# Attention's exponential on VectorE with five equally weighted terms and one V, more buffers for its bits, and the MLP's x plus bias formed on GpSimd

## The chip, the cores and the metric

One Trainium2 chip, one core. The metric is the device time of one execution in microseconds (us), of which the median over several runs counts.

## What is computed

Tokens x (1 x 2048 x 512) go through a layer norm; the result feeds two branches in parallel, and their outputs are added to x:

```python
xn = _layernorm(x, axis=-1)
return x + _A_ref(xn, A_wqkv, A_wo) + _B_ref(xn, B_w1, B_b1, B_w2, B_b2)
```

A is softmax attention with 32 heads of 16 columns (scores scaled by 1/4, no mask), B is an MLP that norms xn once more, 512 to 1792 columns with a tanh GELU, and back to 512 with bias b2.

## The kernel before

**Tiles and groups.** The 32 heads make 8 sets of 4 (HS), the 2048 queries 4 blocks of 512 (QW). A pair of query block and head set is a group g; there are 32 (NG), taken in order. In a group there are 16 key tiles k of 128 keys, and for each k and each of the 4 heads one unit: the scores of 128 keys by 512 queries, one PSUM bank. 32 x 16 x 4 = 2048 units.

**Two engines for the exponential.** TensorE computes scores (`qk`, L1054), for 2 or 3 units in one go that fill banks 0 to 3 in turn. ScalarE takes the exponential of such a tile in one instruction (`fex`, L1237) into `p_sb`, and TensorE multiplies it with V (`pv`, L1072), four heads side by side in the columns of the array: four matmuls of 128 x 32 weights, called a pack below. V has a column of ones per head, so the softmax sum comes out with the product. A further unit can ride along with a tile's scores into another bank (`ride`); it belongs to VectorE. `build_dve` makes the instructions: `f1` (L1319) adds LEVEL to scaled scores, clips at 0 and writes int16, whose bits read as f16 are a rough exponential; `f2` (L1343) adds a constant SHIFT[t] to the bits of all four heads of a key tile, four times, which shifts the place where the roughness lies. The five f16 arrays are multiplied with V and with four copies of V that are scaled by WEIGHT[t] (`vs`, written in `scaled`, L938), and all five products add up in the group's PSUM bank. So a key tile on VectorE costs four `f1`, four `f2` and 20 value matmuls, where one on ScalarE costs four.

**Which unit goes where.** KD lists the key tiles that may go to VectorE: (2, 5, 8, 11, 14) of each group from g = 2 on. `next_d` hands one over when fewer than OUT tiles are under way; what VectorE doesn't take, ScalarE takes at the group's end (`take_unit`). In groups 0 and 1, which run beside the projections, only tile 8 of group 1 goes to VectorE.

**Buffers.** `ib` has NI = 3 slots for a key tile's converted scores, all in `x_sb`, whose tokens are no longer needed; `tb` has NTB = 3 slots for shifted bits. All of them pass in turn.

**The rest.** Keys, queries and V are projected on the way (`project`, `vmm`); for the key tiles of KD but tile 5 the V projection is computed a second time, later, only to write `vs`. Per query block the MLP runs as `build_mlp` (up, bias on VectorE at L1498, GELU on ScalarE at L1508) and `build_down`: per 128 tokens a chain of 16 steps on TensorE through `chain` (L597), one that adds the tokens by a product with the identity, 14 for w2, and one that adds b2 as ones times a row; VectorE copies the result to the accumulator `acc` (L1531, in the memory of `wkv`). `build_out` multiplies the normalised heads with wo, adds `acc` (L1553) and stores. GpSimd has little: constants, the square roots of the norm, and per group four small instructions (L1398 to L1404) that check the softmax sums when they come back from memory as `lc`.

**What sets the order.** No engine chooses at run time. A planner in the program (`_Plan.run`) holds for every operation a cost, a due time (`prio`) and its dependencies, and writes out one fixed order per engine: of the operations that could start, the one due first. Groups are due RATE + 1.1 us apart. In gaps of TensorE's plan it inserts matmuls with zeros (`fill`, L1630), which keep its clock up. A change of a cost, of a slot count or of RATE so moves instructions everywhere.

## Time and profile before

| what | value |
|---|---|
| time, median of 3 runs (lowest to highest) | 817.85 us (816.5 to 818.91) |
| profiled execution, span from first to last instruction | 814.1 us |
| the same execution's own time, by the median's distance | some 3.75 us above its span |
| instructions | 23268 |

The profile is of one execution of its own. Its span runs from the first to the last instruction; what lies around the span isn't in it. Busy time of TensorE is modelled, since matmuls overlap; instructions of VectorE and ScalarE also overlap at their ends, so that the mean of one is longer than the distance from one to the next.

### The profile page before, as it was taken

What the parts mean: (1) busy time and instruction counts of PE and PEld (TensorE: products, weight loads), DVE (VectorE), ACT (ScalarE), POOL (GpSimd) and SP (SyncE); (2) the same over time, 40 slices, a digit from 0 to 9 for tenths busy, and PEclk for the clock granted to TensorE, in tenths of its full rate; (3) what the DMA queues carried; (4) which work ended last, traced back from release to release, by engine and by line L of the source; (5) the groups of instructions that cost most, each with busy time, mean ns of one, the idle gap of its engine ahead of it and who ended that gap; (6) DMA issues with size and microseconds to landing.
All of it is one profiled execution on the core that took longest, in us unless ns stands there. A gap on an engine that the chain in (4) does not pass through costs nothing.

```text
span 814.1 us, 23268 instructions
## 1 busy us (share of the span) xinstructions
PE 780.0 (96%) x9887; PEld 260.7 (32%) x9888; DVE 751.4 (92%) x1304; ACT 775.5 (95%) x676; POOL 57.5 (7%) x165
## 2 busy tenths in 40 slices
PE   8999999999999999999999999999999999999997
PEld 3333332333332333333333333233332333333332
DVE  8959999997899999997999999899899999999885
ACT  6779999999999999999999999899999999999995
POOL 3300001001000000000000000000100010000001
PEclk9999999999999999999999999999999999999999
DMA  6210031101010011200002011100000101211001
GB/s 188 92 22 2 18 84 30 35 15 30 15 30 15 25 45 41 54 22 10 16 16 40 23 35 42 48 21 22 23 16 16 28 16 41 61 42 28 12 23 34
DMA packets 54798, 27.99 MB, mean 34 GB/s; under 512 B 40613, under 2 KB 50598, under 8 KB 54690
## 3 DMA queue, kind: packets, MB, share of 16 engines
q1 hardware_dynamic: 52818, 25.03, 11.3%
q8 instruction: 78, 1.28, 0.7%
q10 hardware_dynamic: 1872, 1.44, 0.6%
q14 instruction: 30, 0.25, 0.1%
HBM read 23.85 MB, written 2.61 MB: 32 GB/s over the span
## 4 chain that ended last, share of the span: by engine, by line
DVE 42%; PE 40%; ACT 10%; issue 7%; DMA 1%; DVEq 0%; ACTq 0%; SPq 0%
DVE x_sb L1319 16%; PE ps L597 14%; PE ps L1072 13%; PE ps L1054 12%; DVE tb_x L1343 10%; ACT p_sb L1237 8%; DVE x_sb L1343 4%; DVE ht L1498 2%; DVE osb L1377 1%; DVE stats L728 1%; ACT ht L1508 1%; DVE qc L918 1%; PE ps L1630 1%; DVE qz L923 1%; DMA ldram<-osb 1%
## 5 line engine op out<-in xcount | busy, mean ns | idle before, releaser
L1237 ACT ACTIVATE p_sb<-ps 128x1024 bf16<-128x1024 f32 (+1 forms) x649 | 734.0, 1251 | 21.6 <-PE ps L1054 10.2
L1054 PE MATMUL ps<-qz,kt 32*128 32x512 bf16 x2048 | 311.0, 383 | 18.6 <-ACT p_sb L1237 6.5
L1319 DVE TENSOR_SCALAR x_sb<-ps 128x512 int16<-128x512 f32 x456 | 301.1, 680 | 21.1 <-PE ps L1054 19.5
L1343 DVE TENSOR_SCALAR tb_x<-x_sb 128x2048 int16<-128x2048 int16 x304 | 202.5, 680 | 1.8 <-PE ps L1072 1.2
L1054 PEld LDWEIGHTS <-kt 32*128 32x128 bf16 x2048 | 85.0, 91 | 276.3 <-issue 269.4
L1072 PE MATMUL ps<-p_sb,va 128*32 128x512 bf16 x1592 | 157.4, 390 | 0.3 <-DVE osb L1377 0.3
L1072 PE MATMUL ps<-tb_x,vs 128*32 128x512 f16 x1216 | 111.7, 382 | 1.1 <-DVE tb_x L1343 0.9
L1343 DVE TENSOR_SCALAR x_sb<-x_sb 128x2048 int16<-128x2048 int16 x152 | 103.5, 681 | 4.1 <-PE ps L1072 3.5
L1072 PEld LDWEIGHTS <-va 128*32 128x32 bf16 x2048 | 49.7, 93 | 107.2 <-issue 103.9
L1072 PEld LDWEIGHTS <-vs 128*32 128x32 bf16 x1824 | 50.3, 96 | 44.1 <-issue 23.6
L1398 POOL TENSOR_SCALAR okt<-lc 128x16 f32<-128x16 f32 x31 | 11.3, 363 | 701.2 <-DMA lc<-ldram 701.2
L597 PE MATMUL ps<-yT,w_r 128*32 128x512 bf16 x896 | 59.2, 384 | 1.6 <-DVE ht L1498 0.8
L1072 PE MATMUL ps<-x_sb,vs 128*32 128x512 f16 x608 | 59.6, 381 | 0.7 <-DVE x_sb L1343 0.6
L597 PE MATMUL ps<-w_sb,ht 128*32 128x512 bf16 x896 | 59.6, 380 | 0.0
L1072 PE MATMUL ps<-x_sb,va 128*32 128x512 f16 x456 | 45.1, 385 | 1.5 <-DVE x_sb L1319 1.2
L1498 DVE TENSOR_SCALAR ht<-ps,b_sb 128x512 bf16<-128x512 f32 x56 | 41.4, 739 | 2.3 <-PE ps L597 2.2
L1630 PE MATMUL ps<-ones_bf,zeros_bf 128*32 128x512 bf16 x416 | 36.8, 384 | 0.0
L597 PE MATMUL ps<-wo_pad,ont 128*32 128x512 bf16 x512 | 33.9, 380 | 0.5 <-DVE ont L1427 0.2
L597 PEld LDWEIGHTS <-w_r 128*32 128x32 bf16 x896 | 22.7, 96 | 25.6 <-issue 11.5
L597 PEld LDWEIGHTS <-ht 128*32 128x32 bf16 x896 | 21.7, 96 | 21.7 <-issue 5.7
L1508 ACT ACTIVATE ht<-ht 128x3584 bf16<-128x3584 bf16 x8 | 25.1, 3183 | 0.0
L1377 DVE COPY osb<-ps 128x512 f32<-128x512 f32 x31 | 21.1, 680 | 0.5 <-PE ps L1072 0.3
(100 smaller groups left out, 362.3 us busy)
## 6 DMA issues: line engine op xcount, KB each, us to landing
rlb<-rdram SPq DMA_DIRECT2D x31, 256.0 KB
w_r<-in_B_w_dram SPq DMA_DIRECT2D x56, 128.0 KB
x_r<-in_A_x_dram SPq DMA_DIRECT2D x16, 128.0 KB
w_sb<-in_B_w_dram SPq DMA_DIRECT2D x1, 1792.0 KB
out_dram<-ot SPq DMA_DIRECT2D x12, 128.0 KB
x_sb<-in_A_x_dram SPq DMA_DIRECT2D x2, 512.0 KB
wkv<-in_A_wqkv_dram ACTq DMA_DIRECT2D x1, 512.0 KB
x_sb<-in_A_x_dram ACTq DMA_DIRECT2D x1, 512.0 KB
```

What stands on the lines that cost most here:

```text
L597: I(nc.tensor.matmul(dst[32 * j:32 * j + 32], lhsT=lhsT[:, 32 * j:32 * j + 32], rhs=rhs, start=start, stop=stop, tile_position=(0, 32 * j)))
L728: I(nc.vector.bn_stats(out=stats[:, t, :], in_=x_sb[:, t, :]))
L1054: I(nc.tensor.matmul(ps[:, bank, :], lhsT=kt[lo:lo + 32, s // 2, k * P:(k + 1) * P], rhs=qz[lo:lo + 32, (qt * NB + s // 2) % NQB, s % 2, : ...
L1072: I(nc.tensor.matmul(ps[32 * j:32 * j + 32, o_bank[g], :], lhsT=vals[:, h * VS:h * VS + 32], rhs=wts(j), start=pv_done[g] == 1, stop=end, ...
L1237: I(nc.scalar.activation(p_sb[:, s0:s1, :].rearrange("p a b -> p (a b)"), ps[:, b0:b0 + n, :].rearrange("p a b -> p (a b)"), AF.Exp, scale ...
L1319: I(nc.vector.tensor_scalar(out=ib[sl][:, j, :], in0=ps[:, pool.bank(key), :], scalar1=LEVEL, scalar2=0.0, op0=ALU.add, op1=ALU.max))
L1343: I(nc.vector.tensor_scalar(out=tb[x].rearrange("p j q -> p (j q)"), in0=ib[sl].rearrange("p j q -> p (j q)"), scalar1=float(SHIFT[t]), sc ...
L1377: e0 = add("DVE", dve(QW), lambda: I(nc.vector.tensor_copy(osb[:, i2, :], ps[:, o_bank[g], :])), pvs + before, pr - 1000, rel=(o_done(g),))
L1398: I(nc.gpsimd.tensor_scalar(out=okt[:, 0, :], in0=lc[:, i2, :], scalar1=L_MIN, scalar2=None, op0=ALU.is_ge))
L1498: I(nc.vector.tensor_scalar(out=ht[:, fc, :], in0=ps[:, misc.bank(key), :], scalar1=b1_sb[:, fc:fc + 1], scalar2=None, op0=ALU.add))
L1508: I(nc.scalar.activation(out=hv, in_=hv, func=AF.Gelu_apprx_tanh, scale=1.0))
L1630: I(nc.tensor.matmul(ps[32 * j:32 * j + 32, o_bank[opened], :], lhsT=zeros_bf[:, 0:32], rhs=ones_bf[:], start=False, stop=False, tile_posi ...
```

## The change

It does four things. The five terms of VectorE's exponential get the same weight, with other shifts, so all five multiply the same V: `vs`, its constants, its second V projections and its copies go. The slots become 5 for converted scores (1 new, 4 in `x_sb`) and 7 for shifted bits, and the slot is the one that comes free first (`ib_free`); `next_d` allows four tiles under way and waits until a slot is about to be free. KD lists seven key tiles. In the down projection, x plus b2 is formed on GpSimd into `acc`, two matmul steps go, and VectorE adds the product to `acc`. Besides, the value matmuls of VectorE's tiles may no longer be the ones that open a group's bank while another is held (`o_late`), the MLP's first product depends on the loaded b1 and the last group's final products on `h_use`, b2 is loaded as 128 equal rows, and RATE falls from 23.75 to 23.25.

```diff
-SHIFT = (0, 205, 410, 614, 819)
-WEIGHT = (1.0, 0.8671875, 0.7578125, 0.65625, 0.57421875)
-LEVEL = 1024.0 * (15.0 - 2.3761451780166682)
+SHIFT = (0, 170, 320, 544, 798)
+LEVEL = 1024.0 * (15.0 - 2.7628058563328386)
...
-    KD = (2, 5, 8, 11, 14)
+    KD = (2, 4, 6, 8, 10, 12, 14)
...
-    NPU, NI, NTB, NON, NW1 = 15, 3, 3, 11, 4
+    NPU, NI, NTB, NON, NW1 = 15, 5, 7, 11, 4
...
-    tb_x = const.tile([P, 2, HS, QW], I16, name="tb_x")
-    ib = [xb[:, n] for n in range(NI)]
-    tb = [tb_x[:, 0], tb_x[:, 1], xb[:, NI]]
+    it = const.tile([P, NI + NTB - 4, HS, QW], I16, name="it")
+    ib = [it[:, n] for n in range(NI - 4)] + [xb[:, n] for n in range(4)]
+    tb = [it[:, NI - 4 + n] for n in range(NTB)]
...
-    vs = const.tile([P, TERMS - 1, len(KD), VROW], BF, name="vs")
...
-    OUT, OPEN, RES, RESL, SLK, ALP = 3, 2, 36, 28, 55.0, 0.0
+    SLOT = 1.0
+    PEND = _Op()
+    OUT, OPEN, RES, RESL, SLK, ALP = 4, 2, 36, 28, 55.0, 0.0
...
-    RATE, QO, PO, AO, DO = 23.75, 50.0, 44.5, 40.0, 14.5
+    RATE, QO, PO, AO, DO = 23.25, 50.0, 44.5, 40.0, 14.5
...
-    ld_b2 = dma("SP", b2_sb[0:1, :], B_b2[None, :], (ld_w2, mk_b2), prio=62.0, lat=4.0)
+    ld_b2 = dma("SP", b2_sb[:], bass.AP(B_b2.tensor, B_b2.offset, [[0, P], [1, D]]), (ld_w2,), prio=62.0, lat=4.0)
...
-    def scaled(pool, key, t, e, pr):
-
-        for n in range(TERMS - 1):
-            def fe(n=n):
-                I(nc.vector.tensor_scalar(
-                    out=vs[:, n, KD.index(t), 0:H * VS].rearrange("p (h r) -> p h r", r=VS)[:, :, 0:DH],
-                    in0=ps[:, pool.bank(key), :].rearrange("p (h r) -> p h r", r=DH),
-                    scalar1=WEIGHT[n + 1], scalar2=None, op0=ALU.mult))
...
-        if t in VSE:
-            scaled(early, key, t, va_op[t], pr - VSP)
-    for i, t in enumerate(KD):
-        if t in VSE:
-            continue
-        pr = ts_(1, 0.2 + 0.2 * i)
-        key = ("vs", t)
-        scaled(misc, key, t, chain(key, pr, vmm(t), (xt_op[t], ld_wv), nb=pr - 8)[1], pr - 350)
...
+    def o_late(key, take=False, give=None):
+        if key not in o_bank and o_held:
+            return None
+        return o_ready(key, take, give)
...
-        if len(todo) >= OPEN or d_busy[0] >= OUT:
+        if len(todo) >= OPEN or d_busy[0] >= OUT or ib_free() is None:
...
+    def ib_free():
+
+        at = {n: max([o.end + o.lat if o.done else 1e9 for o in ib_use.get(n, ())] or [0.0])
+              for n in range(NI)}
+        n = min(at, key=lambda n: (at[n], n))
+        return n if at[n] <= I.now + SLOT else None
...
-            rows.append((vs[:, t - 1, KD.index(k), :], bits(tb[x])))
+            rows.append((va[:, k, :], bits(tb[x])))
...
-            steps = [(ident_bf[:], x_r[:, qi % 2, :])]
-            steps += [(ht[:, fc, cs], w2_sb[:, fc, :]) for fc in range(FC)]
-            steps += [(ones_bf[:, 0:P], b2_sb[:])]
...
+            xb_ = add("POOL", 0.8, lambda c=c, qi=qi: I(nc.gpsimd.tensor_tensor(
+                out=acc[:, c, :], in0=x_r[:, qi % 2, :], in1=b2_sb[:], op=ALU.add)),
+                [xr, ld_b2] + wait, pr - 5)
+            x_use[qi] = (xb_,)
+            steps = [(ht[:, fc, cs], w2_sb[:, fc, :]) for fc in range(FC)]
+            m = chain(key, pr, steps, [gl, ld_w2, xb_])[1]
...
-            acc_op[c] = add("DVE", dve(D), lambda c=c, key=key: I(nc.vector.tensor_copy(
-                acc[:, c, :], ps[:, misc.bank(key), :])),
-                [m] + wait, pr - 500, rel=(one, misc.giver(key)))
+            acc_op[c] = add("DVE", dve(D), lambda c=c, key=key: I(nc.vector.tensor_tensor(
+                out=acc[:, c, :], in0=ps[:, misc.bank(key), :], in1=acc[:, c, :], op=ALU.add)),
+                [m, xb_], pr - 500, rel=(one, misc.giver(key)))
```

Three places of the new order follow. The first is VectorE in the first stage, where the copy of V (L956, now L935) is followed by the scaled copies; statistics and normalised tokens of later blocks (L728, L754) stand around them. Before:

```order
L900 CAST kt<-ps 128x512
L754 TENSOR_SCALAR yT<-x_sb,mv,r_83 128x512
L728 BN_STATS stats<-x_sb 128x6
L729 BN_AGGR mv<-stats 128x2
L956 CAST va<-ps 128x32x16 x2
L938 TENSOR_SCALAR vs<-ps 128x32x16 x4
L956 CAST va<-ps 128x32x16
```

In the change:

```order
L891 CAST kt<-ps 128x512
L746 TENSOR_SCALAR yT<-x_sb,mv,r_83 128x512
L720 BN_STATS stats<-x_sb 128x6
L721 BN_AGGR mv<-stats 128x2
L935 CAST va<-ps 128x32x16 x2
L720 BN_STATS stats<-x_sb 128x6
L721 BN_AGGR mv<-stats 128x2
L935 CAST va<-ps 128x32x16
```

The four scaled copies are gone, and the next statistics stand in their place; up to there the two orders are the same.

The second is GpSimd while the first query block's MLP runs: the four checks of a group's sums, then the next group's. Before (the cast makes a constant):

```order
L1404 TENSOR_TENSOR okall<-okall,okt 128x16
L714 CAST ident_f<-ident_bf 128x128
L1398 TENSOR_SCALAR okt<-lc 128x16
L1400 TENSOR_SCALAR okt<-lc 128x16
L1402 TENSOR_TENSOR okt<-okt 128x16
```

In the change, where the checks are L1375 to L1381:

```order
L1381 TENSOR_TENSOR okall<-okall,okt 128x16
L1501 TENSOR_TENSOR wkv<-x_r,b_sb 128x512 x2
L1375 TENSOR_SCALAR okt<-lc 128x16
L1377 TENSOR_SCALAR okt<-lc 128x16
L1379 TENSOR_TENSOR okt<-okt 128x16
L1381 TENSOR_TENSOR okall<-okall,okt 128x16
L1501 TENSOR_TENSOR wkv<-x_r,b_sb 128x512 x2
```

The additions of x and b2 (L1501, into `acc`) stand two and two between the checks of neighbouring groups.

The third is VectorE at the first eviction of the second query block's down projection. Before:

```order
L1391 TENSOR_TENSOR ont<-osb,rlb 128x512
L1343 TENSOR_SCALAR x_sb<-x_sb 128x2048
L1531 COPY wkv<-ps 128x512
L1343 TENSOR_SCALAR tb_x<-x_sb 128x2048
L1319 TENSOR_SCALAR x_sb<-ps 128x512
```

In the change, where `f1` is L1299, `f2` L1321 and `it` holds the new slots:

```order
L1321 TENSOR_SCALAR it<-x_sb 128x2048 x2
L1299 TENSOR_SCALAR x_sb<-ps 128x512
L1321 TENSOR_SCALAR it<-x_sb 128x2048 x4
L1368 TENSOR_TENSOR ont<-osb,rlb 128x512
L1299 TENSOR_SCALAR it<-ps 128x512
L1509 TENSOR_TENSOR wkv<-ps,wkv 128x512
```

The copy has become an add, and with seven slots four additions of one key tile can stand in a row.

## Rows read from the trace of the kernel before

**Rows 1.** The page's head and part 1, busy time of each engine.

```profile
span 814.1 us, 23268 instructions
...
PE 780.0 (96%) x9887; PEld 260.7 (32%) x9888; DVE 751.4 (92%) x1304; ACT 775.5 (95%) x676; POOL 57.5 (7%) x165
```

**Rows 2.** Stretches: from:to, length, busy us (instructions) per engine, clock, DMA.

```profile
13.50:76.00 62.50, 59.35 (x903) 22.25 (x896) 52.22 (x102) 52.79 (x58) 7.82 (x11) 1.00 0.15 43
76.00:804.00 728.00, 704.59 (x8856) 231.47 (x8859) 684.13 (x1163) 715.77 (x610) 42.52 (x125) 1.00 0.11 29
```

**Rows 3.** Part 4 of the page, shares of the chain that ended last.

```profile
DVE 42%; PE 40%; ACT 10%; issue 7%; DMA 1%; DVEq 0%; ACTq 0%; SPq 0%
```

**Rows 4.** The exponentials: page part 5, then groups of instructions by form.

```profile
L1237 ACT ACTIVATE p_sb<-ps 128x1024 bf16<-128x1024 f32 (+1 forms) x649 | 734.0, 1251 | 21.6 <-PE ps L1054 10.2
...
L1237 ACT ACTIVATE p_sb<-ps 128x1536 bf16<-128x1536 f32 x294 | 436.6, 1485 | 5.8 <-PE ps L1054 4.4
L1237 ACT ACTIVATE p_sb<-ps 128x1024 bf16<-128x1024 f32 x355 | 370.6, 1057 | 15.8 <-PE ps L1072 8.0 <-PE ps L1054 5.8 <-ACT p_sb L1237 0.3
```

**Rows 5.** VectorE's conversions and additions, groups by form.

```profile
L1319 DVE TENSOR_SCALAR x_sb<-ps 128x512 int16<-128x512 f32 x456 | 301.1, 680 | 21.1 <-PE ps L1054 19.5
L1343 DVE TENSOR_SCALAR tb_x<-x_sb 128x2048 int16<-128x2048 int16 x304 | 202.5, 680 | 1.8 <-PE ps L1072 1.2
...
L1343 DVE TENSOR_SCALAR x_sb<-x_sb 128x2048 int16<-128x2048 int16 x152 | 103.5, 681 | 4.1 <-PE ps L1072 3.5
```

**Rows 6.** Pieces of the chain that ended last: start us, us, what.

```profile
355.29 1.20 DVE x_sb L1319 x2
...
127.11 1.20 DVE tb_x L1343 x2
```

**Rows 7.** The scaled copies of V (L938), VectorE's busy time by stretch.

```profile
0.00:76.00 76.00, 7.44 (x12) 1.00 0.28 81
76.00:804.00 728.00, 5.30 (x8) 1.00 0.11 29
```

**Rows 8.** The chain again, in the first stage.

```profile
30.09 2.40 DVE vs L938 x4
...
45.62 3.69 PE ps L597 x64
```

**Rows 9.** TensorE's matmuls that add b2 (those with x alike), by form.

```profile
L597 PE MATMUL ps<-b_sb,ones_bf 128*32 128x512 bf16 x64 | 6.2, 379 | 0.0
```

**Rows 10.** GpSimd's groups by form.

```profile
L1398 POOL TENSOR_SCALAR okt<-lc 128x16 f32<-128x16 f32 x31 | 11.3, 363 | 701.2 <-DMA lc<-ldram 701.2
...
L801 POOL MEMSET b_sb<- 128x512 bf16 x1 | 0.5, 527 | 0.0
...
L714 POOL CAST ident_f<-ident_bf 128x128 f32<-128x128 bf16 x1 | 0.3, 290 | 0.0
```

**Rows 11.** Timeline at 134 us, VectorE and GpSimd: start us, us, engine, what.

```profile
134.48 0.68 DVE L1343 TENSOR_SCALAR tb_x<-x_sb 128x2048 int16<-128x2048 int16 x1
134.51 1.30 POOL L1398 TENSOR_SCALAR okt<-lc 128x16 f32<-128x16 f32 x1 [20.51 <-DMA lc<-ldram]
...
135.08 0.68 DVE L1343 TENSOR_SCALAR x_sb<-x_sb 128x2048 int16<-128x2048 int16 x1
```

**Rows 12.** Timeline at 190 us, the same columns.

```profile
189.55 0.69 DVE L1319 TENSOR_SCALAR x_sb<-ps 128x512 int16<-128x512 f32 x1 [0.82 <-PE ps L1054]
...
190.04 0.25 POOL L1398 TENSOR_SCALAR okt<-lc 128x16 f32<-128x16 f32 x1 [29.95 <-DMA lc<-ldram]
...
190.28 0.71 DVE L1343 TENSOR_SCALAR x_sb<-x_sb 128x2048 int16<-128x2048 int16 x1
```

**Rows 13.** VectorE's copy and its add with the accumulator, groups by form.

```profile
L1531 DVE COPY wkv<-ps 128x512 f32<-128x512 f32 x16 | 11.0, 689 | 8.1 <-PE ps L597 8.1
...
L1553 DVE TENSOR_TENSOR wkv<-ps,wkv 128x512 f32<-128x512 f32 x4 | 2.7, 682 | 1.5 <-PE ps L597 1.5
```

**Rows 14.** Timeline of ScalarE from 400 us, its longest run.

```profile
399.12 44.22 ACT L1237 ACTIVATE p_sb<-ps 128x1024 bf16<-128x1024 f32 x39
```

More of the change, by code (lines that the diff above doesn't have):

```diff
@@ L704 @@
     mk_mask = add("DVE", 0.45, c_mask, (mk_id,), -90)
-    def c_vs(n):
-        def fn():
-            I(nc.gpsimd.memset(vs[:, n, :, 0:H * VS].rearrange("p t (h r) -> p t h r", r=VS)
-                               [:, :, :, DH:VS], WEIGHT[n + 1]))
-            I(nc.gpsimd.memset(vs[:, n, :, H * VS:VROW], 0.0))
-        return fn
-    mk_vs = [add("POOL", 0.43, c_vs(n), (), -80 + n) for n in range(TERMS - 1)]
     mk_half = add("POOL", 0.2, lambda: I(nc.gpsimd.memset(mhalf[:], -0.5)), (), -95)
@@ L932, in vmm @@
                 for jc in range(JC)]
-    def scaled(pool, key, t, e, pr):
-        for n in range(TERMS - 1):
-            def fe(n=n):
-                I(nc.vector.tensor_scalar(
-                    out=vs[:, n, KD.index(t), 0:H * VS].rearrange("p (h r) -> p h r", r=VS)[:, :, 0:DH],
-                    in0=ps[:, pool.bank(key), :].rearrange("p (h r) -> p h r", r=DH),
-                    scalar1=WEIGHT[n + 1], scalar2=None, op0=ALU.mult))
-            rel = (pool.giver(key),) + ((one,) if pool is misc else ())
-            e = add("DVE", dve(QW), fe, (e, mk_vs[n]), pr, rel=rel if n == TERMS - 2 else ())
-        vs_op[t] = e
     for t in range(NT):
@@ L1106, in next_d @@
                 k = left_d[g][0]
-                if not (k in vs_op and vs_op[k].done and kt_op[0, k // TQ].done):
+                if not (va_op[k].done and kt_op[0, k // TQ].done):
                     continue
@@ L1301, in begin @@
             build_down(g // NS, build_mlp(g // NS))
-    ib_use, tb_use = {}, {}
-    tb_n, ib_n = [0], [0]
+    ib_use, tb_use = {NI - 4 + n: x_free[n] for n in range(4)}, {}
+    tb_n = [0]
+    def ib_free():
[3 more added lines that the diff above has]
+        return n if at[n] <= I.now + SLOT else None
     def build_dve(g, k):
-        n_ = ib_n[0]
-        ib_n[0] += 1
-        sl = n_ % (NI if stream["u"] > NU2 // 2 else NFI)
+        sl = ib_free()
         dl = dl_now[0] + 4.0
         ins = []
+        before = list(ib_use.get(sl, ()))
+        ib_use[sl] = [PEND]
         pv_need[g] += TERMS
@@ L1320, in f1 @@
                                           scalar1=LEVEL, scalar2=0.0, op0=ALU.add, op1=ALU.max))
-            o = add("DVE", dve(QW), f1, list(ib_use.get(sl, ())) + x_free[sl],
+            o = add("DVE", dve(QW), f1, before,
                     dl + m - 800.0, hold=1)
@@ L1333, in dve_terms @@
         deps = list(ins)
-        uses = []
+        uses, adds, first_o = [], [], None
         for t in range(1, TERMS):
             x = tb_n[0] % NTB
-            if x == 2 and not all(o.done for o in x_free[3]):
-                x = tb_n[0] = 0
             tb_n[0] += 1
@@ L1346, in f2 @@
                     scalar2=None, op0=ALU.add))
-            a = add("DVE", dve(HS * QW, 0.26), f2, ins + list(tb_use.get(x, ())) + (x_free[3] if x == 2 else []), dl + t - AO - F2)
+            a = add("DVE", dve(HS * QW, 0.26), f2, ins + list(tb_use.get(x, ())), dl + t - AO - F2)
+            adds.append(a)
+            uses.append(x)
+            rows.append((va[:, k, :], bits(tb[x])))
             deps.append(a)
-            rows.append((vs[:, t - 1, KD.index(k), :], bits(tb[x])))
-            uses.append(x)
             if len(rows) == 2 or t == TERMS - 1:
                 o = add("PE", pen(len(rows)), lambda rows=rows: pv(g, k, rows),
-                        deps + [va_op[NT - 1] if g > 1 else va_op[k], vs_op[k]], dl + 5.0 - DO, acq=((o_ready, g),),
+                        deps + [va_op[NT - 1] if g > 1 else va_op[k]], dl + 5.0 - DO, acq=((o_late, g),),
                         mode="p")
@@ L1358, in dve_terms @@
                 rows, deps, uses = [], [], []
-                last_adds = a
-                first_o = o if t == 1 else first_o
-        ib_use[sl] = (last_adds, first_o)
+                first_o = first_o or o
+        ib_use[sl] = (a, first_o)
     ont_use, on_op, osb_use, rlb_use = {}, {}, {}, {}
@@ L1581, in build_final @@
             acq = ((pool, key),) if c else ((one, key), (misc, key))
-            dep = [acc_op[c], mk_idf] + ([exp_prev[0]] if c else [])
+            dep = [acc_op[c], mk_idf] + h_use + ([exp_prev[0]] if c else [])
             if c % 2 == 0:
```

14 lines of the change are left out of this document (5 added, 9 removed).

## The prediction

> **What bounds the kernel now.** The first line of the page gives the span, 814.1 us, and part 1 under it the loads [rows 1]: TensorE 780.0 us busy, VectorE 751.4, ScalarE 775.5. No engine stands far ahead of the others, so the next view must say who waits. The stretches do [rows 2]: from 76 to 804 us, where groups 2 to 31 run, ScalarE is busy 715.8 of 728 us and VectorE 684.1, which leaves VectorE 43.9 us idle and ScalarE 12.2. From 13.5 to 76 us, where groups 0 and 1 run beside the projections, ScalarE is busy 52.8 of 62.5 us: that stage is fed too slowly. The chain that ended last [rows 3] walks mainly over VectorE (42%) and TensorE (40%), over ScalarE only 10%. So ScalarE has the work that is hardest to shrink, but the hand-overs that end late are those of VectorE and TensorE. The idle time that stands behind the groups confirms it: ScalarE's exponential waits 10.2 us for scores and 8.0 us for a value matmul that frees its buffer [rows 4], VectorE's conversion 19.5 us for scores [rows 5]. The exponentials themselves [rows 4] are 649 instructions, 294 over 1536 and 355 over 1024 columns, so 294 x 3 + 355 x 2 = 1592 units of 512 columns, busy 734.0 us: 0.461 us a unit. The other 456 of the 2048 units go to VectorE [rows 5], each as one conversion of 512 columns (L1319) and, per four units, four additions over 2048 columns (L1343), so one of each kind a unit. Two in a row take 1.20 us [rows 6], 0.60 us each, for either kind.
>
> **Step 1, the split of the units.** The built order of the change has 290 exponentials over 1536 columns and 353 over 1024: 1576 units, 16 fewer; VectorE has 472. The first stage keeps its 124 ScalarE units (two groups of 64 less one key tile), so all 16 fall in the long stretch. 16 x 0.461 = **-7.4 us** on ScalarE [rows 4]. I count it whole, since ScalarE has 12.2 us of idle in 728 there [rows 2]: a shorter stretch must come from fewer units.
>
> **Step 2, VectorE's side of it.** Added: 16 conversions and 16 additions, 32 x 0.60 = +19.2 us. Removed: the scaled copies of V, 20 instructions at L938 [rows 7]; four of them take 2.40 us [rows 8], so 20 x 0.60 = -12.0 us. Net +7.2 us. 12 of the 20 lie before 76 us and 8 behind it [rows 7], so the long stretch gets 19.2 - 4.8 = +14.4 us. Its cover is the 43.9 us of idle there [rows 2]; after the stretch has become 7.4 us shorter, 43.9 - 14.4 - 7.4 = 22.1 us of it are left. I count 0. If that cover cannot be used, because those idle pieces are hand-overs, up to +14.4 us show.
>
> **Step 3, the first stage.** The four scaled copies of tile 5 stand at 30.09 us on the chain, between the copy of V and the matmuls that ScalarE waits for [rows 8]. In the new order nothing takes their place: statistics, which stood behind them, move up. **-2.4 us.** The eight copies that follow until 76 us lie where VectorE waits, and their V projections, computed a second time for four tiles, go too: 16 packs of four matmuls. A run of 16 packs takes 3.69 us [rows 8], 0.23 us a pack. I count nothing more for them, though up to 16 x 0.23 = 3.7 us could show, since this stage hangs on TensorE (that run is on its chain).
>
> **Step 4, TensorE.** Gone: 64 matmuls of the second V projection, 64 that add the tokens and 64 that add b2 to the down projection [rows 9]. Added: 64 value matmuls (16 units become 5 x 16 terms in place of 16) and 16 that only fill. -112 matmuls are 28 packs, 28 x 0.23 = -6.4 us of work. On the path it is worth between nothing and TensorE's share of the chain, 0.40 x 6.4 = 2.6 us [rows 3]; I take **-1.0 us**, nearer to nothing, because the order has fill matmuls before and after (104 and 108 packs), so TensorE has places where it waits.
>
> **Step 5, the additions on GpSimd.** 16 instructions, x plus b2 over 128 x 512, bf16 in and f32 out. The trace has none like it. Nearest below is a write alone of 128 x 512, 0.527 us; a cast of 128 columns takes 0.290 [rows 10]. With two inputs I take about twice the write, an estimate of 1.0 us, and 0.53 and 1.1 us as bounds. In the order each stands about one group (24 us) ahead of the VectorE instruction that needs it; no matmul waits for it. GpSimd idles 701.2 us in front of one line alone [rows 10], so its own time is hidden. What is not hidden is what it shares with VectorE. At 134.51 us a GpSimd instruction over 16 columns, which takes 0.25 us elsewhere, lasts 1.30 us, as long as two VectorE additions of 2048 columns run, and ends as the second does [rows 11]. The reverse stands at 190.28 us: the addition was due 0.60 us after the conversion of 189.55, at 190.15, and starts at 190.28, when the GpSimd instruction of 190.04 (0.25 us) ends [rows 12]. So the two exclude each other, and a 1.0 us instruction on GpSimd may hold up VectorE's next addition. Additions fill 472 x 0.60 = 283 us of some 805, 35%; often a conversion of 0.60 us lies between, which goes on. I take 0.4 us of delay for each, 16 x 0.4 = 6.4 us on VectorE, and of that VectorE's share of the chain, 0.42 [rows 3]: **+2.7 us**. Bounds: 0, and 16 x 1.1 = +17.6 us.
>
> [...]
>
> The eviction behind it changes from a copy of PSUM to an add with the accumulator: 0.689 against 0.682 us in rows of either kind [rows 13]; nothing. One more edit has one answer: b2 is loaded once as 128 rows, and nothing is near that waits for it; nothing.
>
> **Step 6, slots and due times.** Five slots for VectorE's converted scores in place of three, seven for the shifted ones in place of three, four sets under way instead of three, candidates at seven key tiles instead of five, and a group is due every 23.25 + 1.1 us instead of 23.75 + 1.1. None of these does work; they let VectorE run ahead. Waits of VectorE for a slot are small now: 3.5 and 1.2 us [rows 5]. I count 0 and make the rest a rival.
>
> **Sum:** -7.4 - 2.4 - 1.0 + 2.7 = -8.1 us. The profiled execution spans 814.1 us; the median of the runs is 817.85, 3.75 us more, which I keep as what lies around the span. 806.0 + 3.75 = 809.75, so **809.7 us**. Its own range is 804 to 814.
>
> **The rivals.**
> A. *The slots decouple the engines.* ScalarE's best long run, 39 exponentials or 97 units in 44.22 us [rows 14], is 0.456 us a unit. If all 1576 ran so, that is 1576 x 0.005 = 7.9 us less, and if its 18.2 us of waits for TensorE [rows 4] halve, there is another 9. Half of all this comes to -8.5, 801 us. For it: three slots for four additions a tile must make VectorE wait for matmuls. Against it: those waits measure under 5 us. Chance 0.2.
>
> B. *VectorE's extra work shows.* The chain runs 42% over VectorE [rows 3], and its idle comes in pieces of about 1 us that wait for scores, which extra slots behind them don't remove. If half of the 14.4 us of step 2 shows, -8.1 + 7.2 = -0.9: 817 us, no change. This is also the case in which the change doesn't do what it says. Chance 0.13.
>
> C. *The lock between GpSimd and VectorE costs more than all else gains (slower).* Place: the 16 additions, in four clusters of four. Without step 5 the sum is -10.8. If each addition stops VectorE, and TensorE behind it in its fixed order, for d us on the path, the change is 16 d - 10.8: it turns slower at d = 0.68 us, and by 3.2 us at 0.88; at 1.1 us it is +6.8, 824.6 us. Against it: at 190.28 the loss was 0.13 us, and conversions don't stop. [...] Chance 0.09.
>
> **How the numbers follow.** Forecast 0.58, A 0.20, B 0.13, C 0.09. The range must leave out no more than 2 in 10: it goes down to A's half-way case, 800.5, and up to B, 817; C and A's far end are left out. A measurement of this kernel can tell 0.3%, 2.5 us, from no change. Faster by more: forecast and A, 0.78 less a hundredth for the forecast's upper tail, 0.77; within: B, 0.13; slower: C and that hundredth, 0.10.
>
> **What the profile of the changed kernel would show.** Step 1: 643 exponentials, near 0.46 us a unit, and the stretch to the end shorter by some 7 us. Step 2: VectorE's idle in it near 22 us. Step 3: the third group starting 2 to 4 us earlier. Step 5: 16 GpSimd rows of 1.0 us or more (longer where VectorE adds), each with at most one VectorE addition starting late by less than 1 us. The prediction is wrong if ScalarE's time per unit moves by more than 0.01 us in either direction (1576 x 0.01 = 15.8 us, more than all steps together), or if VectorE waits behind GpSimd for over 0.7 us an add.

## The result and the profile after

The change took 824.87 us (822.61 to 832.17, 4 runs) beside 817.17 for the kernel before (815.0 to 818.91): ratio 1.0114, interval 1.0067 to 1.0161. It is **slower by 7.7 us**, where the prediction had 8.1 less and a range that ended at 817. A second measurement of the same kernel gave 826.28, ratio 1.0111 [1.0094, 1.0128]; the experiments below are compared with that one, by their ratios to the kernel before. The profile below is of the fastest execution of the first four (822.61 us).

The head of the page and the first line of its chain part, after, to be set beside [rows 1, 3]:

```profile
span 820.8 us, 22955 instructions
PE 775.5 (94%) x9775; PEld 256.7 (31%) x9776; DVE 762.9 (93%) x1316; ACT 771.6 (94%) x670; POOL 76.7 (9%) x172
...
DVE 55%; PE 29%; ACT 7%; DMA 4%; issue 4%; SPq 0%; DVEq 0%; ACTq 0%
```

TensorE and ScalarE have less work than before, VectorE 11.5 us more: 7.2 us as step 2 has it, and 4.3 us that are gone when GpSimd's additions are short (run e1 below, 758.6 us). The chain has moved: VectorE from 42% to 55%, and DMA from 1% to 4%. The costliest groups of the same page (busy time, mean of one in ns, idle before and what ended it), to be set beside [rows 4, 5]:

```profile
L1210 ACT ACTIVATE p_sb<-ps 128x1024 bf16<-128x1024 f32 (+1 forms) x643 | 730.1, 1238 | 32.6 <-PE ps L1027 20.3
L1299 DVE TENSOR_SCALAR x_sb<-ps 128x512 int16<-128x512 f32 x376 | 248.9, 679 | 15.6 <-PE ps L1027 15.4
L1321 DVE TENSOR_SCALAR it<-x_sb 128x2048 int16<-128x2048 int16 x376 | 246.6, 683 | 1.1 <-PE ps L1045 0.3
...
L1501 POOL TENSOR_TENSOR wkv<-x_r,b_sb 128x512 f32<-128x512 bf16 x16 | 20.5, 1289 | 131.6 <-DMA x_r<-in_A_x_dram 90.3
```

The exponentials got 3.9 us cheaper in busy time, and ScalarE's waits for scores doubled (20.3 against 10.2 us). The stretch table, whose columns are the busy time of each engine (with instructions), the granted clock and the DMA, and the row of the copies of the groups' sums (`osb`, first and last start):

```profile
13.50:76.00 62.50, 59.98 (x907) 22.38 (x908) 49.81 (x97) 54.12 (x59) 7.82 (x11) 1.00 0.16 44
76.00:804.00 728.00, 693.06 (x8647) 225.10 (x8643) 694.12 (x1174) 704.05 (x597) 63.84 (x141) 0.99 0.11 29
```

```profile
L1354 DVE COPY osb<-ps x31: 674/682/693, 73.7 to 792.2; 128x512 f32<-128x512 f32 x31
```

The same row before:

```profile
L1377 DVE COPY osb<-ps x31: 670/680/692, 75.4 to 782.1; 128x512 f32<-128x512 f32 x31
```

So the first stage gained 1.7 us, the long stretch between the first and the last copy lost 11.8 (718.5 us in place of 706.7), and what follows the last copy became 3.4 us shorter (28.6 us of the span in place of 32.0). That makes the 6.7 us between the two spans. Whether work at the end was saved or only stands ahead of the last copy now is not shown. In the 728 us from 76 to 804 ScalarE is now busy 704.1 us where [rows 2] has 715.8, and VectorE 694.1 where it has 684.1. No engine became full; the time was lost in waits of one engine for another.

### The profile page after: what moved, and what is told of

It is laid out like the page before. It is cut to its first block, busy times and chain, and to the rows that moved or that the text cites. A ratio compares the mean times of both kernels' runs of the same rounds, so it can differ in the third digit from the quotient of the medians.

```text
span 820.8 us, 22955 instructions
## 1 busy us (share of the span) xinstructions
PE 775.5 (94%) x9775; PEld 256.7 (31%) x9776; DVE 762.9 (93%) x1316; ACT 771.6 (94%) x670; POOL 76.7 (9%) x172
## 4 chain that ended last, share of the span: by engine, by line
DVE 55%; PE 29%; ACT 7%; DMA 4%; issue 4%; SPq 0%; DVEq 0%; ACTq 0%
DVE it L1321 20%; DVE x_sb L1299 17%; PE ps L595 10%; PE ps L1045 10%; PE ps L1027 8%; ACT p_sb L1210 7%; DVE it L1299 4%; DMA ldram<-osb 3%; DVE ht L1475 3%; DVE osb L1354 2%; DVE stats L720 1%; DVE ont L1368 1%; DMA lc<-ldram 1%; DVE qc L909 1%; DVE ot L1531 1%
## 5 line engine op out<-in xcount | busy, mean ns | idle before, releaser
L1210 ACT ACTIVATE p_sb<-ps 128x1024 bf16<-128x1024 f32 (+1 forms) x643 | 730.1, 1238 | 32.6 <-PE ps L1027 20.3
L1299 DVE TENSOR_SCALAR x_sb<-ps 128x512 int16<-128x512 f32 x376 | 248.9, 679 | 15.6 <-PE ps L1027 15.4
L1321 DVE TENSOR_SCALAR it<-x_sb 128x2048 int16<-128x2048 int16 x376 | 246.6, 683 | 1.1 <-PE ps L1045 0.3
L1045 PE MATMUL ps<-it,va 128*32 128x512 f16 x1984 | 166.0, 385 | 3.0 <-DVE it L1321 2.8
L1045 PEld LDWEIGHTS <-va 128*32 128x32 bf16 x3936 | 87.2, 95 | 160.6 <-issue 134.3
L1299 DVE TENSOR_SCALAR it<-ps 128x512 int16<-128x512 f32 x96 | 64.1, 679 | 3.3 <-PE ps L1027 3.2
L1375 POOL TENSOR_SCALAR okt<-lc 128x16 f32<-128x16 f32 x31 | 14.5, 469 | 560.2 <-DMA lc<-ldram 560.2
L1321 DVE TENSOR_SCALAR it<-it 128x2048 int16<-128x2048 int16 x96 | 65.8, 703 | 0.4
L1045 PE MATMUL ps<-x_sb,va 128*32 128x512 f16 x376 | 37.3, 386 | 2.0 <-DVE osb L1354 1.1
L1501 POOL TENSOR_TENSOR wkv<-x_r,b_sb 128x512 f32<-128x512 bf16 x16 | 20.5, 1289 | 131.6 <-DMA x_r<-in_A_x_dram 90.3
L1354 DVE COPY osb<-ps 128x512 f32<-128x512 f32 x31 | 21.2, 684 | 1.6 <-PE ps L1045 1.1
```

Source lines behind the costliest of these rows:

```text
L1045: I(nc.tensor.matmul(ps[32 * j:32 * j + 32, o_bank[g], :], lhsT=vals[:, h * VS:h * VS + 32], rhs=wts(j), start=pv_done[g] == 1, stop=end, ...
L1210: I(nc.scalar.activation(p_sb[:, s0:s1, :].rearrange("p a b -> p (a b)"), ps[:, b0:b0 + n, :].rearrange("p a b -> p (a b)"), AF.Exp, scale ...
L1299: I(nc.vector.tensor_scalar(out=ib[sl][:, j, :], in0=ps[:, pool.bank(key), :], scalar1=LEVEL, scalar2=0.0, op0=ALU.add, op1=ALU.max))
L1321: I(nc.vector.tensor_scalar(out=tb[x].rearrange("p j q -> p (j q)"), in0=ib[sl].rearrange("p j q -> p (j q)"), scalar1=float(SHIFT[t]), sc ...
L1354: e0 = add("DVE", dve(QW), lambda: I(nc.vector.tensor_copy(osb[:, i2, :], ps[:, o_bank[g], :])), pvs + before, pr - 1000, rel=(o_done(g),))
L1375: I(nc.gpsimd.tensor_scalar(out=okt[:, 0, :], in0=lc[:, i2, :], scalar1=L_MIN, scalar2=None, op0=ALU.is_ge))
```

## The experiments

**1. Two suspects, alone and together.** The trace after shows two new things. First, the additions on GpSimd (L1501) meet VectorE's additions (L1321). In the order of time, with start, duration, and number in a run:

```profile
319.51 2.25 DVE L1321 TENSOR_SCALAR it<-it 128x2048 int16<-128x2048 int16 x2
319.69 1.52 POOL L1501 TENSOR_TENSOR wkv<-x_r,b_sb 128x512 f32<-128x512 bf16 x1 [11.64 <-DMA x_r<-in_A_x_dram]
...
365.81 2.71 POOL L1501 TENSOR_TENSOR wkv<-x_r,b_sb 128x512 f32<-128x512 bf16 x2 [10.32 <-DMA x_r<-in_A_x_dram]
365.96 1.55 DVE L1321 TENSOR_SCALAR it<-it 128x2048 int16<-128x2048 int16 x1
```

An addition that is 0.68 us in the trace stands there with 1.55; two that take 1.28 take 2.25. Second, VectorE waits for the softmax sums at the reciprocal, 5.0 us in 5 places where it was 1.8 in one. The waits table (line, what it waited for, total us, times, longest), after and then before, and the chain from 152 to 165 us in order of time:

```profile
DVE rc L1361 <- DMA lc<-ldram: 5.0, 5, 2.4
```

```profile
DVE rc L1384 <- DMA lc<-ldram: 1.8, 1, 1.8
```

```profile
152.81 0.36 DVE ht L1475
153.17 6.60 DMA ldram<-osb
159.77 0.02 SPq L1358
159.80 0.05 issue
159.84 1.54 DMA lc<-ldram
...
161.47 0.25 DVE rc L1361
161.73 0.57 DVE ht L1475
162.30 0.61 DVE x_sb L1299
```

The trip of the sums, from the issue of their store to that of the load that brings them back, took 1.7 to 1.8 us in 27 of 31 groups before and in 18 after, and over 4 us in 1 before and in 10 after. The edits of four runs, one line each:

```diff
 e1: out=acc[:, c, 0:16], in0=x_r[:, qi % 2, 0:16], in1=b2_sb[:, 0:16], op=ALU.add
 e2: I(nc.vector.reciprocal(rc[:, i2, :], mhalf[:]))     # in place of lc[:, i2, :]
 e3: both;  e7: the edit of e2 in the kernel before
```

> The changed kernel with its 16 GpSimd additions cut from 512 to 16 columns (x plus b2 is left out of the other columns); every engine's order stays as it is, so only the time in which GpSimd excludes VectorE goes. In the profile of the change the additions of VectorE that met one lasted 4 to 5 us longer in all. Theory V (VectorE sets the pace, so its net 7.2 us of work and the lock show nearly in full): 4 to 5 us faster than the change. Theory L (the lock's stalls pass on to TensorE and ScalarE and are the main cause): 10 us or more faster than the change, no slower than before. Theory W (waits of VectorE for the softmax sums): within 2 us of the change.

> The changed kernel with VectorE's reciprocal of the softmax sums taken of a constant in place of the sums, so that it doesn't wait for their way through memory (the division by the sums is left out); every engine's order stays. In the change five of these waits last 5.0 us in all, the longest 2.4 us, against 1.8 us before. Theory V: 1 to 3 us faster than the change. Theory L: the same as the change within 2 us. Theory W (these waits stop VectorE, and TensorE and ScalarE behind it, and are the main cause): 5 us or more faster than the change.

> The changed kernel with both edits of the runs before: 16-column additions on GpSimd, and no wait for the softmax sums; all orders as they are. Alone they took 5.3 and 8.4 us off the change. If they are two causes: 12 to 15 us faster than the change, 0.992 to 0.997 of the kernel before. If they are one chain (a late VectorE is what makes the sums late): no more than 9 us faster than the change, 1.000 or above.

> The kernel before with the reciprocal taken of a constant, so without VectorE's wait for the softmax sums (the division by them is left out). There one of 31 trips through memory is late (4.9 in place of 1.8 us). Theory W (the change made ten of these trips late): 0 to 2 us faster than the kernel before. If the wait costs as much in any order: 6 to 9 us faster than the kernel before.

| run | median us | ratio to before, interval |
|---|---|---|
| change, again | 826.28 | 1.0111 [1.0094, 1.0128] |
| e1, short additions | 820.22 | 1.0046 [1.0027, 1.0064] |
| e2, no wait for sums | 817.29 | 1.0008 [0.999, 1.0026] |
| e3, both | 814.56 | 0.9965 [0.9952, 0.9978] |
| e7, before, no wait for sums | 813.84 | 0.9962 [0.9948, 0.9976] |

In ratios, e1 is 0.0065 below the change, 5.3 us; e2 0.0103, 8.4 us; both together 0.0146, 11.9 us. The two overlap: alone they make 13.7. The wait for the sums costs the kernel before 3.1 us. So both suspects are real, and the net of them against the kernel before is 11.9 - 3.1 = 8.8 of the 9.1 us. What is left of the change without them is e3 against e7: +0.3 us, with an error of some 1.6. That is the second puzzle: for the rest, steps 1 to 4 and 6, the prediction had -10.8.

**2. The down projection alone.** The equally weighted terms and the slots of the change with the x and b2 steps on TensorE as before, on the plan that comes out.

```diff
-            xb_ = add("POOL", 0.8, ... acc[:, c, :], in0=x_r[:, qi % 2, :], in1=b2_sb[:], op=ALU.add)
+            steps = [(ident_bf[:], x_r[:, qi % 2, :])]
...
+            steps += [(ones_bf[:, 0:P], b2_sb[:])]
```

> The changed kernel with the down projection as before: tokens and b2 added by matmuls, VectorE copies, nothing of it on GpSimd; the order is planned anew. TensorE gets 32 packs back (32 x 0.23 = 7.4 us). Theory V: VectorE loses 4 to 5 us of lock, so 0 to 5 us faster than the change. Theory L: 8 us or more faster. Theory T (TensorE sets the pace): 3 to 7 us slower than the change.

822.33 us, 1.0077 [1.0061, 1.0094]: 2.8 us below the change, about half of what the short additions gave. The two matmul steps come back, and the order is planned anew (7 late trips, 464 units on VectorE in place of 472); which of these takes the other half is not shown.

**3. The product ahead of other work.** On VectorE's order, the product of the normalised heads (`ont`) stands two rows or less ahead of the next group's copy of its sums 12 times after and 3 times before. There is one buffer for the broadcast reciprocals (`rlb`), so when the product ends, the next 256 KB broadcast goes out, in group 2 of the change 0.7 us ahead of the store of the sums (116.24 and 116.97 us). These runs give the product an earlier due time (pr - 500), in the change and in the kernel before.

```diff
-            [e3] + list(ont_use.get(g - NON, ())), pr)
+            [e3] + list(ont_use.get(g - NON, ())), pr - 500)
```

> The changed kernel, complete, with one number changed: the product of a group's output with its reciprocal sums on VectorE is due 500 us earlier, so it runs as soon as it can. In the change it stands directly ahead of the next copy of a group's output 12 times (3 before), so that the 256 KB broadcast of reciprocals that it releases leaves 0.7 us ahead of the next sums' 8 KB store; in this order that happens twice. The plan gives VectorE 488 units, ScalarE 1560. Theory W: the sums' trips fall back to 1.8 us and the time to 6 to 14 us below the change's (0.993 to 1.003 of the kernel before). Theory V (VectorE sets the pace): VectorE has 16 units more, 19 us of work, and the time is no better than the change's.

> The same one number in the kernel before; 452 units on VectorE, no product directly ahead of a copy (3 in the kernel before). Theory W: 0 to 3 us faster than the kernel before, since only one trip was late there. If the order of this product matters by itself: 5 us or more either way.

Both missed. e5 took 894.3 us (1.0951 [1.0921, 1.0982]), e6 819.41 (1.0045 [1.0029, 1.006]). In both, late trips all but vanish (1 of 31, and none), and neither is faster. e5's plan ran ahead with the groups (21 copies of sums by 514.0 us, where the change has 19) and then starved: the next copy starts at 659.3 us. Its stretch table:

```profile
76.00:514.00 438.00, 418.14 (x4855) 132.64 (x4851) 435.39 (x746) 431.32 (x374) 39.08 (x89) 1.00 0.09 24
514.00:660.00 146.00, 107.86 (x1220) 38.99 (x1213) 80.07 (x132) 54.71 (x45) 5.65 (x8) 0.79 0.11 27
```

A due time changes the whole plan, so such a run says little about the wait it was meant for.

**4. Which engine sets the pace.** Here the order stays and one engine's instructions become shorter: VectorE's conversions 448 of 512 columns (e9 on e3, e10 on e7), or each exponential 48 columns shorter (e11 on e3, e12 on e7). In e11, e12 and, for one slot of five, e9, zeros are written to these columns once, at the start; elsewhere old bits stay there.

```diff
 e9, e10: tensor_scalar(out=ib[sl][:, j, 0:448], in0=ps[:, pool.bank(key), 0:448], ...)
 e11, e12: activation(p_sb[...][:, 0:n * QW - 48], ps[...][:, 0:n * QW - 48], ...)
```

> The change with short additions on GpSimd and without the wait for the sums (as the run with both), and each of VectorE's 472 conversions 448 columns instead of 512: 64 of 512 columns of every VectorE slot are not computed. VectorE is busy about 31 us less (472 x 64 columns at some 1.04 ns), everything else in the same order. If VectorE's work sets the pace of the long stretch, this is 10 to 20 us below the run with both (ratio to the kernel before 0.972 to 0.984), and more than the same cut gives in the kernel before. If ScalarE sets the pace, it stays within 3 us of it (0.993 to 1.000). If the falls of TensorE's clock hold the time, it follows those: with VectorE ahead fewer waits of TensorE and under 10 us at the lower clock, and 5 to 10 us less.

> The kernel before without the wait for the sums, and each of its 456 conversions on VectorE 448 columns instead of 512 (64 of 512 columns of every VectorE slot are not computed): some 30 us less on VectorE. If VectorE had room in the kernel before, as the prediction counted it (43.9 us idle, cost of 7.2 us more set to 0), the time stays within 2 us of the same kernel with full conversions (ratio 0.993 to 0.999). If VectorE already sets the pace there, 8 to 18 us less (0.974 to 0.986).

> The change with short additions and without the wait for the sums, and each of the 643 exponentials on ScalarE 48 columns shorter (48 of every 512, 1024 or 1536 columns are not computed): some 26 us less on ScalarE, the order kept. If ScalarE sets the pace of the long stretch, as Step 1 of the prediction has it (0.461 us of span for each 0.41 us of work), 15 to 29 us below the run with both (ratio 0.961 to 0.978). If VectorE sets it, at most 3 us (0.993 to 0.999).

> The kernel before without the wait for the sums, and each of its 649 exponentials 48 columns shorter (not computed there): 26 us less on ScalarE. If ScalarE sets the pace before the change, as Step 1 rests on, 15 to 29 us less than the same kernel with full ones (ratio 0.961 to 0.978). If TensorE and VectorE set it, under 5 us (0.990 to 0.998).

e9 took 808.3 us (0.9891 [0.9876, 0.9907]) and e10 805.36 (0.9857 [0.9841, 0.9874]). e11 and e12 took 4923 and 4925 us, since the sums without the tails left the bounds that the program checks, and its general path ran behind the fast one. So all four are read at the last copy of a group's sums, which lies in the fast part. From the tile's rows between 765 and 790 us, the rows of e3, e11 and e9 (L1354), then those of e7, e12 and e10 (L1377):

```profile
L1354 DVE COPY osb<-ps x1: 684/684/684, 784.2 to 784.2; 128x512 f32<-128x512 f32 x1
L1354 DVE COPY osb<-ps x1: 684/684/684, 780.9 to 780.9; 128x512 f32<-128x512 f32 x1
L1354 DVE COPY osb<-ps x1: 684/684/684, 777.4 to 777.4; 128x512 f32<-128x512 f32 x1
...
L1377 DVE COPY osb<-ps x1: 691/691/691, 781.3 to 781.3; 128x512 f32<-128x512 f32 x1
L1377 DVE COPY osb<-ps x1: 691/691/691, 777.9 to 777.9; 128x512 f32<-128x512 f32 x1
L1377 DVE COPY osb<-ps x1: 692/692/692, 771.5 to 771.5; 128x512 f32<-128x512 f32 x1
```

| | last copy, full | cut | gain | busy time cut (costliest group's rows) | gain per us cut |
|---|---|---|---|---|---|
| VectorE, change (e3, e9) | 784.2 | 777.4 | 6.8 | 313.2 - 284.7 = 28.5 | 0.24 |
| VectorE, before (e7, e10) | 781.3 | 771.5 | 9.8 | 301.1 - 273.0 = 28.1 | 0.35 |
| ScalarE, change (e3, e11) | 784.2 | 780.9 | 3.3 | 728.6 - 708.1 = 20.5 | 0.16 |
| ScalarE, before (e7, e12) | 781.3 | 777.9 | 3.4 | 733.9 - 714.2 = 19.7 | 0.17 |

Each number is of one execution. By the median times VectorE's cut gains 6.0 us in the change and 8.6 before, 0.21 and 0.31 for each us. The trace of e7 is of its slowest execution, 1.3 us over the median, so the gains before are some 1 us too large. Neither of these two engines sets the pace alone, and VectorE weighs more. The change does not make it weigh more: the cut gives less there than before. TensorE's work was not cut in this way. What ScalarE saved was mostly taken up by waits for another engine: in e11, its waits for scores rise to 25.6 us, from 14.4 in e3. The 1.04 ns a column of the expectation for e9 agree with two VectorE copies out of PSUM in the trace of before, 680 ns for 512 columns and 160 for 14; measured, e9's cut of 28.5 us is 0.94 ns for each of its 472 x 64 columns.

**5. TensorE's clock.** After the stall of the chain above, the granted clock fell. The stretch table of the change, around it:

```profile
160.00:163.00 3.00, 0.69 (x15) 0.32 (x11) 1.52 (x4) 1.87 (x3) 0.91 (x4) 1.00 0.30 71
163.10:166.40 3.30, 3.30 (x31) 1.00 (x23) 2.89 (x5) 0.96 (x2) 0.00 (x0) 0.50 0.03 6
167.00:170.00 3.00, 3.00 (x50) 1.14 (x54) 2.90 (x5) 2.76 (x3) 0.00 (x0) 1.00 0.00 0
```

TensorE was busy 0.69 of 3.00 us, then its granted clock was 0.50: 31 matmuls in 3.3 us, where later, at 1.00, 50 fit into 3.0. While TensorE was slow, ScalarE was busy 0.96 of 3.30 us. The executions of one and the same kernel go with this clock: those of the change, second measurement, ran from 823.5 us at a mean clock of 0.987 to 831.4 at 0.975. In the traces of before and of the change the granted clock is 1.00 or 0.50, and nothing between. With these two values alone, a mean of 0.012 less is 2 x 0.012 x 827 = 20 us more at 0.50, an estimate, for 7.9 us of time. Over 107 timed executions of 15 kernels (the second measurement of the change and every run after it but e5, e11 and e12), taken within each kernel, it is 0.31 us of time for each us at 0.50, counted in this way (correlation 0.88). By that, the change (mean clock 0.983, so 28 us at 0.50) would lose some 7 us more than the kernel before (0.997, so 5 us), an estimate. A correlation doesn't say whether the fall costs or the stall that goes ahead of it, so two runs put filling matmuls into TensorE's planned gaps, 62 packs in e3 and 72 in e7, with all else in the same order.

```diff
-    NEED = 10.2
+    NEED = 12.2
```

> The change with short additions on GpSimd and without the wait for the sums, and the planner's bound for filling packs raised from 10.2 to 12.2: 62 packs of zero matmuls more in TensorE's planned gaps (some 13 us), every other instruction in the same order. The run without them spends 17.0 us of its body at TensorE's lower clock, where the kernel before without the wait spends none; at half speed that is 8.5 us of work. If these falls took what the fewer ScalarE units gave, they go (under 4 us at the lower clock) and the time falls by 5 to 9 us (ratio to the kernel before 0.985 to 0.991). If the falls only follow stalls that cost the time anyhow, the time stays within 2 us (0.994 to 0.999). If TensorE's work sets the pace, up to 13 us more (to 1.013).

> The kernel before without the wait for the sums, with the same bound for filling packs: 72 packs more (some 15 us). It has no stretch at the lower clock to win back, so this is the price of the fill alone: 0 to 3 us if the packs lie in gaps (ratio 0.996 to 1.000), 10 to 15 us more if TensorE's work sets the pace (1.008 to 1.015). The effect of the clock in the change is the difference between the two pairs.

f1 took 811.57 us (0.9932 [0.9917, 0.9948]), by the ratios 2.7 below e3; f2 814.14 (0.9967 [0.9956, 0.9977]), 0.4 above e7; each difference has an error of some 1.5. The long stretch of e3 and then of f1:

```profile
76.00:800.00 724.00, 697.74 (x8706) 225.72 (x8704) 692.21 (x1180) 706.36 (x600) 48.48 (x141) 0.99 0.11 29
```

```profile
76.00:800.00 724.00, 707.08 (x8979) 229.15 (x8971) 694.67 (x1184) 708.97 (x603) 47.88 (x141) 1.00 0.11 29
```

The mean time at a clock of 0.50 fell from 15.4 to 7.0 us, that is 0.32 us of time for each us, as in the correlation. So some 13 us of added matmuls (62 packs of 0.21 us, an estimate: at 365 us in the trace of the change 8 such matmuls take 0.61 us and 4 take 0.40) made a kernel faster that had falls and left one alone that had none. The falls that went had taken some 3 us of what the change was to give in e3: less than the 5 to 9 that the clock theory expected. With equal fill the change without its two suspects is 2.9 us below the kernel before without the wait (0.9932 against 0.9967), with an error of 1.5. That is what steps 1 to 4 and 6 are worth together with most of the falls gone; no run separates step 6 from the others.

The falls also lie in the prices of the two suspects: the mean time at 0.50 is 27.8 us in the change, 21.1 in e1, 16.4 in e2 and 15.4 in e3. At 0.31, some 3.5 of the 8.4 us that e2 gave go with the falls, an estimate.

**6. The late trips, cured twice.** f3 lets the planner hold a broadcast back while the next group's sums are due or on their trip. f5 keeps the plan and swaps the two on SP's queue alone, 11 times. Both compute the whole. The two rules, in short and not as code:

```text
 f3: rlb: acq=((clear, g),)     clear: None while osb(g + 1) is ready and lc(g + 1) not loaded
 f5: send(g): if osb(g + 1) is ready and lc(g + 1) not loaded, issue rlb(g) right after lc(g + 1)
```

> The change, complete, with one rule more in the planner: the 256 KB broadcast of a group's reciprocals is not issued while the next group's sums are due or on their trip. The trips of the sums should then take 1.7 to 2.3 us in nearly all groups (10 of 31 took over 4 us), and VectorE should not wait at the reciprocal. By the theory that the broadcast issued just ahead makes the trip late, the time falls by 5 to 8 us against the change (ratio to the kernel before 1.001 to 1.006). By the rival that the trip is late whatever goes ahead of it, or that a later product costs as much in wo's block, it stays at 1.009 to 1.013.

> The change, complete, with one difference on SP's queue alone: 11 times the 256 KB broadcast of the reciprocals goes behind the next group's sums (store and load) instead of ahead of them; every other engine has the same instructions in the same order. The run with the broadcast held by the planner had no late trip and gained nothing, but on another plan, with 30 us at the lower clock. If VectorE's stall at the reciprocal (5.0 us, 5 times) is what the run without the wait got back, trips of 1.7 to 2.6 us, no stall, and 5 to 9 us less than the change (ratio to the kernel before 1.000 to 1.005). If what that run got back is something else (the later products, the falls of the clock), the time stays at 1.008 to 1.013 with the stall gone.

f3: 825.47 us (1.01 [1.0078, 1.0122]). f5: 827.6 us (1.0129 [1.0104, 1.0155]). The mechanism of the trips was right. SP's queue in group 2 of the change (start, duration of the issue), then of f5:

```profile
116.24 0.55 SPq L1366 DMA_DIRECT2D rlb<-rdram  x1
116.97 0.51 SPq L1356 DMA_DIRECT2D ldram<-osb  x1
121.36 0.33 SPq L1358 DMA_DIRECT2D lc<-ldram  x1
```

```profile
117.97 0.51 SPq L1369 DMA_DIRECT2D ldram<-osb  x1
119.71 0.32 SPq L1354 DMA_DIRECT2D lc<-ldram  x1
120.12 0.56 SPq L1347 DMA_DIRECT2D rlb<-rdram  x1
```

The store that stands 0.7 us behind the broadcast comes back after 4.4 us, the one ahead of it after 1.7. In f5 and in f3 no trip is over 3 us, and no wait at the reciprocal is left. But the time stays. The waits table of f5, whose trace is of its fastest execution (820.77 us), has a new stall:

```profile
DVE ont L1380 <- DMA rlb<-rdram: 3.8, 2, 2.0
```

The broadcast that was moved back is now the one VectorE waits for, 3.8 us at the product in place of 5.0 at the reciprocal. That this wait takes back all that the other gave is likely, but no run shows it. What f5 does show is that trips in time do not bring the 8.4 us of e2 as long as the broadcast then comes late: e2 frees the reciprocal, and with it the broadcast and the product behind it, from the sums altogether. In f3 VectorE has neither wait, and the clock (mean 0.984) is as low as in the change (0.983), on a plan of its own. In its trace (clock 0.981, that of the change 0.990) the last copy of sums starts at 790.2 us, 2.0 earlier than in the trace of the change, and 34.7 us follow it in place of 28.6: that plan loses at its end more than it had won. Which dependency makes its end longer isn't settled.

**7. The best complete kernel that the parts suggested.** f4 is e4 with the held broadcast, f6 is e4 with the swap and the fill of f1.

> The equally weighted terms and the slots of the change, the down projection of the kernel before (no addition on GpSimd), and the broadcast held back as in the run beside it; complete. If the two causes add up (2.8 us from the additions on GpSimd in that form, 5 to 8 us from the late sums), 814 to 817 us (ratio 0.996 to 1.000), level with the kernel before and not clearly below it. If the plan that comes out has waits of its own, 1.002 to 1.008.

> The equally weighted terms and the slots of the change with the down projection of the kernel before, the broadcast behind the next group's sums on SP, and the planner's bound for filling packs at 12.2; complete. From 822.3 us: stall at the reciprocal gone (2.8 us there, times 1.7 by the two kernels without the wait: 4.8 less), fill 2 to 3 us less: 814 to 817 (ratio 0.995 to 1.000). If the swap does nothing by itself, 1.003 to 1.008.

Both missed the 814 to 817 us that the parts came to. f4: 820.67 us (1.0048 [1.003, 1.0066]), the best complete form of the change, and still slower than the kernel before; its plan gives VectorE 456 units, as many as before the change. f6: 822.7 (1.0065 [1.0052, 1.0078]), 1.0 us below e4, within the error: with the swap and the fill the mean clock is 0.994, from 0.989 in e4, and the two together gave next to nothing. The gain of f1 does not carry over to every plan.

## Why the prediction was wrong

**Step 1 (-7.4) is the term that was mis-sized most.** The split came out as built (643 exponentials, 1576 units, 0.463 us of busy time each). The error is in "I count it whole, since ScalarE has 12.2 us of idle in 728 there". ScalarE, 98% busy (715.8 of 728 us), did not set the pace: runs e11 and e12 took some 20 us off it and got 3.3 and 3.4 us. At 0.17, step 1 is worth 7.4 x 0.17 = 1.3 us, an estimate. The chain had said so: ScalarE had 10% of it [rows 3].

**Step 2 (0) should have cost.** The cover of 43.9 us idle on VectorE [rows 2] could not be used; it was hand-overs, as rival B had it. VectorE's idle time in that stretch is 33.9 us after the change, where the prediction had 22.1. Runs e9 and e10 price VectorE's work at 0.24 to 0.35 us for each us, in the kernel before the higher. The 14.4 us that the step adds to the long stretch come to 3.5 to 5.0 us at that rate, an estimate, and outweigh step 1.

**Step 3 (-2.4):** the first copy of sums came 1.7 us earlier. Right, a little large. **Step 4 (-1.0)** was not separated by any run. Together, at these rates, steps 1 to 4 come to -1.3 + 3.5 (or 5.0) - 1.7 - 1.0 = -0.5 to +1.0; e3 against e7 measured +0.3, and -2.9 with equal fill, where the prediction had -10.8. That the first two agree is partly luck: e3 is 2.9 us behind e7 at the last copy of sums, and gains 3.5 behind it (28.6 against 32.1 us), an end that no step names.

**Step 5 (+2.7) had the mechanism and half the size.** The instruction takes 1.15 us undisturbed, in the median 1.17, and not 1.0; the bound of 1.1, which no row of before shows, is passed as well. The hold-up ran both ways: VectorE's 0.68 us became 1.55, and GpSimd's 1.15 became 1.52. At 319 us VectorE's first addition began ahead of GpSimd's (319.51 and 319.69), and GpSimd's took 1.52 us and VectorE's two together 2.25; at 365 us GpSimd's began ahead (365.81 and 365.96), and VectorE's took 1.55; but at 134.51 us [rows 11] a GpSimd instruction lasted, by the records, through an addition that began after it too. A conversion beside the additions on GpSimd was not longer: 0.69 us at 189.80 us, 0.68 at 367.44. The price is 5.3 us, 0.33 us for each of the 16, falls of the clock included. That is under the 0.68 at which rival C would have turned the sign by itself. C named the right sign with one of the two causes; that its 824.6 us, at 1.1 us for each addition, lies beside the measured 824.87 is luck, since no run shows 1.1 us on the path for each, and the runs showed 0.33.

**Missing altogether: the wait for the sums, +5.3 us net** (8.4 after, 3.1 before). No step or rival follows the chain of store, load, reciprocal, store, broadcast and product through SP's queue. Step 6 counted the due times and slots at 0 because "none of these does work"; they do decide what stands next to what. The rows that would have raised the question were to be had: the built order shows how often the product stands right ahead of the copy of the sums, and the trace of before has one late trip, with a wait of 1.8 us at the reciprocal. They would not have told the price.

The parts make the whole: +0.3 for steps 1 to 4 and 6, +5.3 for step 5, +5.3 for the wait, less the 1.8 by which the two overlap, are the 9.1 us of the second measurement. The 3.75 us that the prediction puts around the span are 1.8 in every execution on record; the profiled execution was some 2 us faster than the median. The forecast, which starts from the median, doesn't change by it.

**The stated tests, and how they are read.** The prediction called itself wrong if ScalarE's time per unit moved by over 0.01 us. As busy time, the figure that stands beside this test, it stayed (0.461 before, 0.463 after). As the time from the first to the last copy of sums for each unit, it moved: 706.7 / 1468 = 0.481 us before and 718.5 / 1452 = 0.495 after. Busy time of one engine could not show what went wrong here. The second test, a wait of over 0.7 us of VectorE behind each addition, is met at the two places shown (0.87 and 0.97) but not on average: 4.3 us over 16 additions are 0.27.

## What to carry to other kernels

Three engines were each over 90% busy here, and neither of the two that were cut set the pace alone. So price a us of work on each by cutting it with the order kept, before work is moved from one to another; here it was 0.16 to 0.17 on ScalarE and 0.24 to 0.35 on VectorE. In a program with a fixed order, read in the built order what now stands next to what, each DMA queue included, and above all whether a large transfer goes out right ahead of a small one that somebody waits for (here 4.4 us in place of 1.7). Taking one stall away can hand it to the next wait of the same chain (here 5.0 us at the reciprocal became 3.8 at the product), so a cure is to be judged by the time, not by the wait that is gone.

## What the hardware showed

The VectorE addition that GpSimd's add held up at 365.96 us starts on time in the records and is only longer, 1.55 in place of 0.68 us; by the gaps between instructions nothing is seen. The load that follows an 8 KB store went out 4.4 us after it where the store stood 0.7 us behind a 256 KB broadcast on the same queue, and 1.7 us after it where the store went first. And some 13 us of matmuls with zeros made a kernel 2.7 us faster, while the time that TensorE spent at a granted clock of 0.50 went from 15.4 to 7.0 us.
